# A convolution and two matrix products with an exponential between: convolutions moved, output rounds redistributed over the product steps

## Chip, cores and metric

One core of a Trainium2 chip. The time is the device time of one execution in microseconds (us); lower is better. Profiled spans are some 2 us shorter than the timed runs.

## The reference

```python
# 1. causal convolution of 7 taps, one softmaxed filter for each of 8 heads of 24 columns
#    x: (8, 4096, 192), weight: (8, 7)  ->  a: (32768, 192)
# 2. h = a @ w_in                       # (32768, 192) @ (192, 2048)
# 3. g = where(h > 0, h, exp(min(h, 0)) - 1)
# 4. out = g @ w_out                    # (32768, 2048) @ (2048, 192), float32
```

## The kernel before

It works through 32 **supersteps** of 1024 rows. A superstep has 16 **product steps**: TensorE multiplies 128 columns of w_in into one of three places in PSUM (H), ScalarE takes the exponential from there, POOL clamps it, VectorE reads the clamp and H and writes g. TensorE may write a place of H again only when VectorE has read it. Between the products TensorE does **output rounds** (two matmuls on g and w_out, side by side, from the two halves of its rows) and the **convolutions** (two for a superstep, each in two halves; each takes a place of H in turn as a product does). Outputs of half a superstep, 64 rounds, gather in one pair of banks, `ops`, which ScalarE evicts. A run of rounds has one of two sides (`turned`): which half of TensorE's rows writes which of the two banks. Before a change of side the rounds wait for the run before. In the cut below, `LAG` says at which step the rounds of a half begin, counted from the end of its superstep (-3: step 13, and step 5 of the next superstep for the other half), and each bracket of `GAPS` holds the rounds after one product.

```python
LAG = -3
GAPS = ((10,), (10,), (6,), (6,), (10,), (5, 6), (11,))   # rounds after the products of a half
CONV_AT = ((2, 1, 1), (10, 2, 0))                        # step, supersteps ahead, which convolution
EARLY_CONV = {3: (1, 0), 6: (1, 1), 9: (2, 0)}           # the first ones, by product
X_AT = ((3, 2, 1), (8, 2, 0), (11, 3, 2))                # row loads for the convolutions

    def take_slot(what):                 # the three places of H, in turn
        k = len(prior)
        prior.append(occupant[k % 3])
        occupant[k % 3] = what
        return k
# ... TensorE:
            def wait_slot(k):
                was = prior[k]
                if was is None:
                    return
                if was[0] == "h":
                    W(s_tt, 2 * was[1] + 2)        # VectorE has read that product
                else:
                    conv_read(W, was[1])
# ... TensorE, output rounds:
                                if runs[prev][0][1] != turned:
                                    W(s_swap, 2 * (prev + 1))
# ... POOL:
                for u in range(2):
                    W(s_exp, 2 * n + u + 1)
                    g.tensor_scalar(
                        out=E[:, n % NE, u, :], in0=E[:, n % NE, u, :],
                        scalar1=1.0, scalar2=0.0, op0=ALU.min, op1=ALU.max,
                    ).then_inc(s_clp)
```

Of the kernel before, what the change touches and what calls it, by code (L numbers as in the profile page):

```python
# [21 lines left out]
WPG = 5  # L22
HB = 2
BN = HB * CPH * 2 * WPG
GAP_SPLIT = 4
TAP = 6
GS = 512
SUP = 2 * GS
# [1 line left out]
NXB = 2  # L30
NE = 4
NG3 = 2
LAG = -3
GAPS = ((10,), (10,), (6,), (6,), (10,), (5, 6), (11,))
WCOLS = ((0, 256), (256, 640), (640, 1280), (1280, 2048))
Q_PART = (0,) * 2 + (1,) * 3 + (2,) * 5 + (3,) * 6
WARM = (9, 1)

CONV_AT = ((2, 1, 1), (10, 2, 0))
EARLY_CONV = {3: (1, 0), 6: (1, 1), 9: (2, 0)}  # L40
FREE_CONV = 3
QUAD = 4
XTW = 136
HALO = 2
X_AT = ((3, 2, 1), (8, 2, 0), (11, 3, 2))
X_LATE = (17, 3, 2)


def bass_lightweight_conv__then__act_elu_kernel(
# [17 lines left out]
    NS = NT // SUP  # L67
# [10 lines left out]
    def take_slot(what):  # L78
# [4 lines that stand above are left out]

    order = []

    def conv_at(s, g, gap=None):
        m = 2 * s + g - 2
        if m >= FREE_CONV:
            slot_of_conv[m] = take_slot(("c", m))
        order.append(("c", m, 0))  # L90
        between = []
        if gap:
            between, gap[:] = gap[:GAP_SPLIT], gap[GAP_SPLIT:]
        if between:
            order.append(("o", between))
        order.append(("c", m, 1))
# [4 lines left out]
    for t in range(NS):  # L101
        for half in range(2):
            at, turned = [0, 0], 0
            for i, sizes in enumerate(GAPS):
                n = NQ * (t + 1) + LAG + 8 * half + i
                gaps = []
# [28 lines left out]
    for n in range(NP):  # L135
        s, i = divmod(n, NQ)
        slot_of_pair[n] = take_slot(("h", n))
        order.append(("h", n))
        gaps = list(rounds_at.get(n, ()))
        if len(gaps) == 2:  # L140
            order.append(("o", gaps.pop(0)))
        if n in EARLY_CONV:
            conv_at(*EARLY_CONV[n])
        if s:
            for at, ahead, g in CONV_AT:
                if at == i and s + ahead < NS:
                    conv_at(s + ahead, g, gaps[0] if gaps else None)
        if gaps and gaps[0]:
            order.append(("o", gaps[0]))
    last_slot = [take_slot(None) for _ in range(2)]  # L150
    order.append(("o", tail))

# [35 lines left out]
    with ExitStack() as stack:  # L188
# [108 lines left out]
        def conv_bank(m):  # L297
            return ops if m < FREE_CONV else H[:, slot_of_conv[m] % 3, :].rearrange(
                "p (b t) -> p b t", b=2
            )  # L300
# [7 lines left out]
        def conv_read(W, m):  # L308
            W(s_ce, m + 1)
# [24 lines left out]
        @block.gpsimd  # L334
        def _gpsimd(g: bass.BassGpSimd):
            W = Waits(g)

            def load_x(s, part):
                b, t0 = s % NXB, s * SUP
                first = s % SPB == 0  # L340
                if part == 0 and not first:
                    return
                if part == 0:
                    W(s_x[b][0], x_need[s, 0])
                    g.memset(xg[0:PAD, b, 0, :], 0.0).then_inc(s_z)
                    return
                if s > NXB:
                    W(s_cv, 2 * (s - NXB))
                row = t0 + GS * (part - 1) - PAD
                v0 = WPG * (part - 1)  # L350
                whole = WPG
                if row + TOK * (WPG - 1) + P > NT:
                    whole = WPG - 1
                    rest = NT - row - TOK * whole
                    g.dma_start(
                        xg[0:rest, b, v0 + whole, :],
                        x_flat[NT - rest : NT, :],
                    ).then_inc(s_xr, 16)
                src = bass.AP(
                    tensor=x_flat.tensor,  # L360
                    offset=row * D,
                    ap=[[D, P], [TOK * D, whole], [1, D]],
                )
                g.dma_start(xg[:, b, v0 : v0 + whole, :], src).then_inc(s_x[b][part - 1], 16)  # L364

            def load_w_in(k, halves):
                c0, c1 = WCOLS[k]
                for r in halves:
                    g.dma_start(  # L369
                        w_in[HP * r : HP * (r + 1), :, c0:c1],  # L370
                        moe_w_in.rearrange("(p j) f -> p j f", j=3)[:, :, c0:c1],
                    ).then_inc(s_w[k], 16)

            W(s_one, 1)
            g.affine_select(
                out=ident[:],
                in_=ident[:],
                pattern=[[-1, P]],
                compare_op=ALU.is_equal,
                fill=0.0,  # L380
                base=0,
                channel_multiplier=1,
            ).then_inc(s_id)
            g.affine_select(  # L384
                out=sel[:].rearrange("p (r h c) -> p r h c", r=2, h=HEADS),
                in_=sel[:].rearrange("p (r h c) -> p r h c", r=2, h=HEADS),
                pattern=[[0, 2], [-1, HEADS], [0, 8]],
                compare_op=ALU.is_equal,
                fill=0.0,
                base=0,  # L390
                channel_multiplier=1,
            ).then_inc(s_id)
            W(s_wd, 16)
            load_w_in(0, (0, 1))
            load_w_in(1, (0, 1))
            load_x(1, 1)
            load_w_in(2, (0, 1))
            load_x(1, 2)
            load_w_in(3, (0,))
            load_x(2, 1)  # L400
            g.dma_start(
                w_out[:, :, :], moe_w_out.rearrange("(q p) d -> p q d", p=FC)
            ).then_inc(s_w[4], 16)
            load_x(2, 2)
            for n in range(NP):
                s, i = divmod(n, NQ)
                for at, ahead, part in X_AT:
                    if at == i and s and s + ahead < NS:
                        load_x(s + ahead, part)
                if n == X_LATE[0]:  # L410
                    load_x(*X_LATE[1:])
                for u in range(2):
                    W(s_exp, 2 * n + u + 1)
                    g.tensor_scalar(  # L414
                        out=E[:, n % NE, u, :],
                        in0=E[:, n % NE, u, :],
                        scalar1=1.0,
                        scalar2=0.0,
                        op0=ALU.min,
                        op1=ALU.max,  # L420
                    ).then_inc(s_clp)

        @block.scalar
        def _scalar(a):
# [57 lines left out]
            def conv_evac(m, b):  # L482
                s, u = m // 2 + 1, m % 2
                h0 = 4 * u + HB * b
                return a.activation(  # L485
                    csb[:, s % 2, :].rearrange(
                        "p (j v h i) -> p h j v i", j=3, v=2 * WPG, h=HEADS
                    )[:, h0 : h0 + HB],
                    conv_bank(m)[:, b, 0:BN].rearrange(
                        "p (h v i j) -> p h j v i", h=HB, v=2 * WPG, j=3  # L490
                    ),
                    ACT.Copy,
                )

            for item in order:
                if item[0] == "c":
# [7 lines left out]
                    conv_evac(m, 0)  # L504
                    if m < FREE_CONV:
                        late.append(m)
# [88 lines left out]
        def _tensor(pe):  # L595
# [16 lines left out]
            def warm_pair(count):  # L612
                for _ in range(count):
                    for r in range(2):
                        pe.matmul(  # L615
                            ops[:, r, :],
                            zw[HP * r : HP * (r + 1), 0:P],
                            zw[HP * r : HP * (r + 1), :],
                            start=True,
                            stop=True,  # L620
                            tile_position=(HP * r, 0),
                        )
# [56 lines left out]
            for x_, item in enumerate(order):  # L679
                if item[0] == "c":  # L680
# [4 lines left out]
                    else:  # L685
# [6 lines left out]
                        W(s_z, z_need[s])  # L692
                        if m < FREE_CONV:
                            conv_read(W, m - 1)
# [22 lines left out]
                elif item[0] == "h":  # L717
                    n = item[1]
                    s, q = divmod(n, NQ)
                    if n == 0:  # L720
                        W(s_ha, 2)
                        W(s_hd, 2)
                    elif n < NQ + LAG and not any(n - 2 <= e < n for e in EARLY_CONV):
                        conv_read(W, sum(e < n for e in EARLY_CONV) - 1)
                        warm_pair(WARM[1])
# [18 lines left out]
                else:  # L744
                    W(s_w[4], 16)
                    for y, (t, half, q, kb, turned) in enumerate(item[1]):
# [3 lines left out]
                        if (x_, y) in run_from:  # L750
# [7 lines left out]
                            else:  # L758
                                conv_read(W, FREE_CONV - 1)
                                W(s_oev, place[key])  # L760
# [93 lines left out]
```

## Time and profile before

Median of the four runs beside the change: 748.59 us (747.39 to 749.51).

| engine | busy, us | share of 746.5 us |
|---|---|---|
| TensorE matmuls | 731.6 | 98% |
| POOL | 664.5 | 89% |
| ScalarE | 646.8 | 87% |
| VectorE | 638.0 | 85% |

With one engine at 98% such a table cannot tell whether its work or its small waits set the time. What can is the distance from one matmul's start to the next, compared with that distance where nothing waits. The prediction shows the lines for it.

### The profile page before, as it was taken

What the parts mean: (1) busy time and instruction counts of PE and PEld (TensorE: products, weight loads), DVE (VectorE), ACT (ScalarE), POOL (GpSimd) and SP (SyncE); (2) the same over time, 40 slices, a digit from 0 to 9 for tenths busy, and PEclk for the clock granted to TensorE, in tenths of its full rate; (3) what the DMA queues carried; (4) which work ended last, traced back from release to release, by engine and by line L of the source; (5) the groups of instructions that cost most, each with busy time, mean ns of one, the idle gap of its engine ahead of it and who ended that gap; (6) DMA issues with size and microseconds to landing.
All of it is one profiled execution on the core that took longest, in us unless ns stands there. A gap on an engine that the chain in (4) does not pass through costs nothing.

```text
span 746.5 us, 28038 instructions
## 1 busy us (share of the span) xinstructions
PE 731.6 (98%) x11866; PEld 505.4 (68%) x11866; DVE 638.0 (85%) x1042; ACT 646.8 (87%) x1224; POOL 664.5 (89%) x1108
## 2 busy tenths in 40 slices
PE   6899999999999999999999999999999999999997
PEld 3466667666766676666766766766766766766666
DVE  5789889889889888898898898898898898888894
ACT  4888988988988988888989989989989989889883
POOL 8799999999899999899999899999999899898893
PEclk9999999999999999999999999999999999999999
DMA  9544435535435535345535345635345444244212
GB/s 168 93 76 91 62 70 93 94 61 92 63 68 94 93 60 95 57 74 95 82 71 94 46 84 94 77 77 70 64 91 94 67 87 81 53 89 81 46 44 66
DMA packets 132881, 58.93 MB, mean 79 GB/s; under 512 B 98068, under 2 KB 132372, under 8 KB 132756
## 3 DMA queue, kind: packets, MB, share of 16 engines
q0 software_dynamic: 44160, 17.28, 22.9%
q1 hardware_dynamic: 88308, 39.37, 21.9%
q8 instruction: 93, 1.52, 0.9%
q10 hardware_dynamic: 288, 0.49, 0.2%
q14 instruction: 32, 0.26, 0.1%
HBM read 35.61 MB, written 25.17 MB: 81 GB/s over the span
## 4 chain that ended last, share of the span: by engine, by line
PE 93%; DVE 2%; POOL 2%; DMA 1%; ACT 1%; issue 0%
PE H L735 45%; PE ops L770 44%; PE H L703 3%; DVE gT L579 2%; DMA xg<-in_x_dram 1%; ACT E L515 1%; POOL E L414 1%; PE H L770 1%; POOL w_in L369 1%; ACT csb L485 0%; POOL xg L364 0%; PE ops L703 0%; ACT osb L474 0%; PE ops L615 0%; POOL sel L384 0%
## 5 line engine op out<-in xcount | busy, mean ns | idle before, releaser
L579 DVE SCALAR_TENSOR_TENSOR gT<-E,H 128x512 f16<-128x512 f32 x1024 | 632.5, 681 | 90.9 <-POOL E L414 84.4
L414 POOL TENSOR_SCALAR E<-E 128x512 f32<-128x512 f32 x1024 | 603.9, 615 | 69.5 <-ACT E L515 62.1
L515 ACT ACTIVATE E<-H 128x512 f32<-128x512 f32 x1024 | 546.2, 608 | 73.5 <-PE H L735 64.8
L770 PE MATMUL ops<-w_out,gT 64*128 64x192 f16 x8064 | 426.4, 243 | 0.3
L770 PEld LDWEIGHTS ops<-w_out,gT 64*128 64x128 f16 x8064 | 346.9, 94 | 110.5 <-ACT osb L474 11.4
L735 PE MATMUL H<-att,w_in 64*128 64x512 bf16 x3072 | 409.2, 378 | 2.9 <-DVE gT L579 1.7
L735 PEld LDWEIGHTS H<-att,w_in 64*128 64x128 bf16 x3072 | 130.9, 94 | 111.7 <-DVE gT L579 12.8
L485 ACT ACTIVATE csb<-H 128x480 bf16<-128x480 f32 x118 | 60.9, 568 | 7.4 <-PE H L703 0.4
L474 ACT ACTIVATE osb<-ops 128x768 f32<-128x768 f32 x63 | 52.0, 826 | 6.2 <-PE ops L770 6.2
L364 POOL DMA_DIRECT2D xg<-in_x_dram x62 | 55.7, 899 | 0.1
L703 PE MATMUL H<-xg,Tm 64*128 64x240 bf16 x472 | 44.0, 263 | 0.1
L703 PEld LDWEIGHTS H<-xg,Tm 64*128 64x128 bf16 x472 | 21.2, 94 | 0.8 <-DVE gT L579 0.3
L485 ACT ACTIVATE csb<-ops 128x480 bf16<-128x480 f32 x6 | 3.5, 588 | 3.2 <-PE ops L703 3.2
L770 PE MATMUL H<-w_out,gT 64*128 64x192 f16 x128 | 5.9, 243 | 0.0
L703 PE MATMUL ops<-xg,Tm 64*128 64x240 bf16 x24 | 2.7, 306 | 3.3 <-DMA xg<-in_x_dram 3.1
L590 DVE COPY osb<-H 128x192 f32<-128x192 f32 x1 | 0.4, 358 | 6.3 <-PE H L770 6.3
L770 PEld LDWEIGHTS H<-w_out,gT 64*128 64x128 f16 x128 | 5.3, 94 | 0.0
L369 POOL DMA_DIRECT2D w_in<-in_moe_w_in_dram x7 | 4.6, 663 | 0.3 <-DMA wh<-in_weight_dram 0.3
L610 PE MATMUL ops<-zw 128*128 128x512 bf16 x9 | 3.6, 577 | 1.2 <-DVE zw L527 1.2
L615 PE MATMUL ops<-zw 64*128 64x512 bf16 x12 | 2.4, 381 | 2.3 <-ACT csb L485 2.3
L703 PEld LDWEIGHTS ops<-xg,Tm 64*128 64x128 bf16 x24 | 0.9, 97 | 5.2 <-issue 3.5
L615 PEld LDWEIGHTS ops<-zw 64*128 64x128 bf16 x12 | 0.6, 93 | 4.2 <-ACT csb L485 3.9
(49 smaller groups left out, 26.3 us busy)
## 6 DMA issues: line engine op xcount, KB each, us to landing
out_dram<-osb SPq DMA_DIRECT2D x126, 192.0 KB, 4.1
xg<-in_x_dram POOLq DMA_DIRECT2D x61, 240.0 KB, 5.6
w_out<-in_moe_w_out_dram POOLq DMA_DIRECT2D x1, 768.0 KB, 16.1
att<-csb SPq DMA_TRANSPOSE x31, 6.4
w_in<-in_moe_w_in_dram POOLq DMA_DIRECT2D x2, 240.0 KB, 9.0
xf<-in_x_dram ACTq DMA_DIRECT2D x1, 384.0 KB, 3.2
xf<-in_x_dram SPq DMA_DIRECT2D x1, 384.0 KB, 3.6
w_in<-in_moe_w_in_dram POOLq DMA_DIRECT2D x2, 144.0 KB, 4.2
```

Source lines behind the costliest of these rows:

```text
L364: g.dma_start(xg[:, b, v0 : v0 + whole, :], src).then_inc(s_x[b][part - 1], 16)
L369: g.dma_start(w_in[HP * r : HP * (r + 1), :, c0:c1], moe_w_in.rearrange("(p j) f -> p j f", j=3)[:, :, c0:c1],).then_inc(s_w[k], 16)
L414: g.tensor_scalar(out=E[:, n % NE, u, :], in0=E[:, n % NE, u, :], scalar1=1.0, scalar2=0.0, op0=ALU.min, op1=ALU.max,).then_inc(s_clp)
L474: a.activation(osb[:, b, :, :, :].rearrange("p g k d -> p g (k d)"), ops[:, :, 0 : 2 * D], ACT.Copy,).then_inc(s_oev)
L485: return a.activation(csb[:, s % 2, :].rearrange("p (j v h i) -> p h j v i", j=3, v=2 * WPG, h=HEADS)[:, h0 : h0 + HB], conv_bank(m)[:, b, ...
L515: a.activation(E[:, n % NE, u, :], H[:, k, GS * u : GS * (u + 1)], ACT.Exp).then_inc(s_exp)
L579: v.scalar_tensor_tensor(out=gT[:, s % NG3, q, u, :], in0=E[:, n % NE, u, :], scalar=1.0, in1=H[:, slot_of_pair[n] % 3, GS * u : GS * (u + ...
L610: pe.matmul(ops[:, 0, :], zw[:, 0:P], zw[:], start=True, stop=True)
L615: pe.matmul(ops[:, r, :], zw[HP * r : HP * (r + 1), 0:P], zw[HP * r : HP * (r + 1), :], start=True, stop=True, tile_position=(HP * r, 0),)
L703: ins = pe.matmul(to[:, b, n1 * hh : n1 * (hh + 1)], Tm[HP * rt : HP * (rt + 1), h, :], xg[HP * rt : HP * (rt + 1), s % NXB, :, :].rearran ...
L735: ins = pe.matmul(H[:, k % 3, GS * r : GS * (r + 1)], w_in[HP * r : HP * (r + 1), j, FC * q : FC * (q + 1)], att[HP * r : HP * (r + 1), s ...
L770: ins = pe.matmul(acc[:, g, d0 : d0 + D], gT[HP * rt : HP * (rt + 1), t % NG3, q, g, t0 : t0 + P], w_out[HP * rt : HP * (rt + 1), q, :], s ...
```

## The change

It is meant to keep apart the two extra jobs of ScalarE, the convolution's eviction and the output's: the convolutions go half way between the output evictions, and the rounds are dealt anew over the steps. (`FREE_CONV` counts the first convolutions, which write `ops` and take no place of H.)

```diff
-LAG = -3
-GAPS = ((10,), (10,), (6,), (6,), (10,), (5, 6), (11,))
+LAG = -4
+GAPS = ((), (8,), (11,), (6, 5, 4), (7,), (1,), (9,), (13,))
-CONV_AT = ((2, 1, 1), (10, 2, 0))
-EARLY_CONV = {3: (1, 0), 6: (1, 1), 9: (2, 0)}
-FREE_CONV = 3
+CONV_AT = ((7, 1, 1), (15, 2, 0))
+EARLY_CONV = {6: (1, 0), 8: (1, 1)}
+FREE_CONV = 2
-X_AT = ((3, 2, 1), (8, 2, 0), (11, 3, 2))
-X_LATE = (17, 3, 2)
+X_AT = ((0, 2, 1), (6, 2, 0), (8, 2, 2))
 ... (in the order of a step)
+        if convs and len(gaps) == 3:
+            order.append(("o", gaps[0]))
+            conv_at(*convs[0], gaps[1])
+            order.append(("o", gaps[2]))
+            continue
```

## The prediction

> **What bounds the kernel now.** I read the page first, then the timeline of one steady half, then the waits, then the start.
>
> ```profile
> span 746.5 us, 28038 instructions
> PE 731.6 (98%) x11866; PEld 505.4 (68%) x11866; DVE 638.0 (85%) x1042; ACT 646.8 (87%) x1224; POOL 664.5 (89%) x1108
> ...
> PE H L735 45%; PE ops L770 44%; PE H L703 3%; DVE gT L579 2%; DMA xg<-in_x_dram 1%; ACT E L515 1%; POOL E L414 1%; PE H L770 1%; POOL w_in L369 1%; ACT csb L485 0%; POOL xg L364 0%; PE ops L703 0%; ACT osb L474 0%; PE ops L615 0%; POOL sel L384 0%
> ```
>
> TensorE is busy 98% and is 93% of the chain, but three engines stand behind it at 85 to 89%. So the question is what TensorE loses inside its own row. The timeline of TensorE shows that (start, length, line, count):
>
> ```profile
> 223.27 1.46 PE L735 MATMUL H<-att,w_in 64*128 64x512 bf16 x12
> 224.56 0.99 PE L770 MATMUL ops<-w_out,gT 64*128 64x192 f16 x20
> 225.39 0.81 PE L735 MATMUL H<-att,w_in 64*128 64x512 bf16 x6
> ...
> 231.44 0.57 PE L770 MATMUL ops<-w_out,gT 64*128 64x192 f16 x10
> 231.85 0.37 PE L703 MATMUL H<-xg,Tm 64*128 64x240 bf16 x4
> 232.10 0.50 PE L770 MATMUL ops<-w_out,gT 64*128 64x192 f16 x8
> 232.44 0.37 PE L703 MATMUL H<-xg,Tm 64*128 64x240 bf16 x4
> ...
> 234.46 1.46 PE L735 MATMUL H<-att,w_in 64*128 64x512 bf16 x12
> ```
>
> Lengths overlap, so I take starts from starts. A product step costs (224.56 - 223.27)/2 = 0.648 us; an output round, two matmuls side by side, (225.39 - 224.56)/10 = 0.0825 us; a half convolution of 4 matmuls 0.205 us, and 0.25 us if the output rounds after it have changed sides (231.85 to 232.10). A half (8 steps, 64 rounds, one convolution) has 8 x 0.648 + 64 x 0.0825 + 0.41 = 10.87 us of work. The two halves from this point take 11.19 (234.46 - 223.27) and 11.31 us, mean 11.25. Loss: 0.38 us a half, over 64 halves 24 us of 749, which is all that a reordering in steady state can win. Who takes it, in the waits of the stretch from 84.4 to 732 us:
>
> ```profile
> PEld ops L770 <- ACT osb L474: 10.7, 58, 0.2
> PEld H L735 <- DVE gT L579: 8.0, 35, 0.4
> ...
> PEld ops L770 <- PE ops L770: 4.3, 25, 0.3
> ```
>
> The first costs nothing: it is a weight load that waits beside the two products of the empty step (after the x12 line the rounds begin 1.29 us later, exactly two products). The second is the real one: a product may start only when VectorE has read what lay in its one of three H places. The third is the change of sides.
>
> The length of that ring decides. Here is one product with every engine behind it free:
>
> ```profile
> 252.95 3.81 DVE L579 SCALAR_TENSOR_TENSOR gT<-E,H 128x512 f16<-128x512 f32 x6
> ...
> 253.29 0.81 PE L735 MATMUL H<-att,w_in 64*128 64x512 bf16 x6
> ...
> 254.15 1.09 ACT L515 ACTIVATE E<-H 128x512 f32<-128x512 f32 x2 [0.39 <-PE H L735]
> ...
> 254.82 1.19 POOL L414 TENSOR_SCALAR E<-E 128x512 f32<-128x512 f32 x2 [0.18 <-ACT E L515]
> ```
>
> Product at 253.29, VectorE done at 252.95 + 3.81 = 256.76: **3.47 us**, and some 0.06 until TensorE restarts, so 3.53. Any stretch of TensorE's order between a product and the one three H places later must last 3.53 us, or TensorE stands. The convolution takes an H place too, which shortens the stretch around it.
>
> **What the Trainium skill says.** "TensorE: Matmul & The Clock Gate", Back-to-back issue gap, gives columns/2.4 + 2.5 ns: 216 ns for 512 and 82.5 for 192. The trace agrees: 1.29/6 = 0.215 and 0.0825 us. So the row is at its rate wherever nothing waits. "PSUM — Partial Sum Buffer", PSUM bank collisions, says that different row tiles may not use one bank at once; that is why rounds that swap sides wait for the run before, and the trace shows that as the 0.25 against 0.205. "Perfetto Trace Analysis", Identifying the Most-Contended Engine, calls matmul busy time a bad metric and prefers the weight loads' share; 68% here, yet only 3.4% of the row can be won, so neither number alone decides and I go by starts. The clock gate section of the first page says that an idle window of about 3.4 us halves the clock; here the table by stretches has the clock at 1.00 from 38.5 us to 732, and 0.94 between 10.8 and 38.5, so it matters at the start alone.
>
> **The change, part by part.** Removed and added work: none in matmuls, evictions or bytes. Every half still has 64 rounds, one convolution, 8 products, 9 runs of rounds. What moves: rounds per step from 10,10,6,6,10,5+4+2,11,0 (steps 13, 14, 15, 0, 1, 2, 3, 4, and again 5 to 12) to 0,8,11,6+5+4,7,1,9,13 (steps 12 to 3, and 4 to 11); the convolution from step 2 to step 15 (10 to 7); the row loads from steps 3 and 11 to 0 and 8.
>
> (1) Convolution. Before, one of its two borders had rounds that change sides; now 6, 5, 4 alternate, so both do: 0.05 + 0.01 us more a half, on the path.
>
> (2) Ring. TensorE's time by step afterwards: step 12: 0.65; 13: 0.648 + 8 x 0.0825 = 1.31; 14: 1.56; 15: 0.648 + 15 x 0.0825 + 0.51 = 2.40; 0: 1.23; 1: 0.73; 2: 1.39; 3: 1.72. Stretches between users of one H place:
> - 0 to 3: 1.23 + 0.73 + 1.39 = 3.35 against 3.53, so 0.17 us is lost whatever the other engines do. Step 1 with its single round is the cause.
> - 12 to 15: 0.65 + 1.31 + 1.56 = 3.52. ScalarE takes product 12 late because it evicts the output just before (the same delay is in the trace: product at 245.77, VectorE done at 249.36, ring 3.59), so 3.65 is needed: short by 0.13.
> - 2 to 5 (the next half's second step, as 13): 1.39 + 1.72 + 0.65 = 3.76; but product 2 follows 1 after only 0.73 us while ScalarE needs 0.97 for one (3.10/3 in the trace) and POOL 1.15, so its ring is 3.93: short by about 0.2, less what earlier standing gives back.
> - 13 to the convolution: 4.01, against 4.08 + 0.06 for the second of two products back to back. 14 to 0, 15 to 1, 1 to 4 and 3 to 6 fit (3.95, 3.62, 3.84, 3.68).
> Carrying each engine's free time from step to step by hand (0.97, 1.15 and 1.20 us a product for ScalarE, POOL and VectorE; 1.02 more where POOL starts a row load; 0.92 and 0.69 on ScalarE for convolution and output) the standing settles at 0.17 + 0.06 + 0.06 + 0.05 = 0.34 us a half. With two changes of sides 0.12, and 0.035 for weight loads that come late, 0.50 against 0.38 before. The same walk on the order of before gives 11.20 for the half measured as 11.19.
>
> So steady state becomes slower: 0.12 x 2 = 0.23 us a superstep, over about 29.5 of them +6.8 us. The memset before each new batch now falls on step 6, where POOL is already late: an estimated 7 x 0.15 = +1. At the end the 6, 5, 4 stand without a convolution between: +0.3.
>
> (3) Start. Here the change gives something back:
>
> ```profile
> 18.33 1.23 PE L703 MATMUL ops<-xg,Tm 64*128 64x240 bf16 x8 [3.05 <-DMA xg<-in_x_dram]
> ...
> 20.10 0.72 SPq L802 DMA_DIRECT2D w_in<-w_in  x1
> ```
>
> Before, the first convolution is at step 3 and TensorE stands 3.05 us for its rows. Now it is at step 6, which VectorE's pace (1.2 us a product after the fourth at 14.45) puts at 18.05, and the rows have landed. But step 10 needs the last columns of w_in, whose copy starts at 20.10 and lands after 6.3 us (table of DMA issues), 26.4. So step 10 starts near 26.4 instead of 28.16; carried on, superstep 1 begins near 35.2 instead of 38.5, with 8 rounds more done (0.66). The wait of 0.82 us in step 19 (two row loads close together) should go too. Together -4.8 us.
>
> Sum: 749.2 + 6.8 + 1 + 0.3 - 4.8 = **752.5 us**.
>
> **The rivals.** (A) The intent works: ScalarE's two extra jobs, now half a half apart, no longer pile up and the ring never closes. For it: ScalarE, POOL and VectorE all lag exactly where both fall together now. Then the loss falls to the changes of sides, 0.12, saving 0.26 x 64 = 17, and with the start it would be about 728 us. Against it: the 3.35 us between 0 and 3 is below the ring with all engines free, so it cannot vanish. (B) A late transfer: the transposition now follows a convolution in step 7 instead of 2. From there to the next superstep there are about 13.8 us; convolution, eviction and the slowest landing (8.3 us) need 11.5. Were it to miss by 1 us, 30 supersteps would make 780. Rows asked for in step 8 have seven steps, as now; they land in 5.5. I hold this unlikely. (C) Only the start counts and the ring is as before: 744.
>
> **Range and chances.** The steady term is uncertain by about 5 us (0.08 us a half, as the halves of before differ by 0.1), the start by 2. So 746 to 758. Faster by 2% means 734, which needs A in full; slower by 2% means 764, which needs B or twice my ring loss.
>
> **What would show it.** In the profile after: halves of 11.3 to 11.4 us where 11.25 was; TensorE's rounds of step 2 followed by a product that waits some 0.17 us for VectorE, in nearly every half; both convolution borders at 0.25; superstep 1 beginning at 35 +- 2 us and no 3 us wait for rows. Wrong if the half is under 11.2, if a wait for the transposition or rows shows in each superstep, or if rounds wait for ScalarE after the empty step.

## The result

754.33 us median (752.03 to 754.69, 4 runs) against 748.59. Ratio 1.0071, interval 1.0045 to 1.0097: 0.7% slower, inside 2%. (A ratio is the mean of one kernel's runs over the mean of the other's of the same rounds, so not quite the ratio of the medians.)

Taking the starts of products from both traces says where the 5.6 us between the profiled spans (746.5 and 752.1) lie:

| stretch | before, us | after, us | difference |
|---|---|---|---|
| start of product 0 to product 32 | 48.47 | 47.62 | -0.85 |
| product 32 to product 496 (29 supersteps) | 653.27 | 659.54 | +6.27 |
| product 496 to the end | 34.02 | 34.24 | +0.22 |

The loss is spread evenly over the steady state: 22.71 us a superstep in the median, in place of 22.51. The timeline of TensorE after the change, one steady half (start, length, line, count):

```profile
222.81 1.48 PE L733 MATMUL H<-att,w_in 64*128 64x512 bf16 x12
...
228.83 0.81 PE L733 MATMUL H<-att,w_in 64*128 64x512 bf16 x6
229.48 0.74 PE L768 MATMUL ops<-w_out,gT 64*128 64x192 f16 x14
230.06 0.81 PE L733 MATMUL H<-att,w_in 64*128 64x512 bf16 x6
230.71 0.25 PE L768 MATMUL ops<-w_out,gT 64*128 64x192 f16 x2
230.79 0.81 PE L733 MATMUL H<-att,w_in 64*128 64x512 bf16 x6
231.44 0.91 PE L768 MATMUL ops<-w_out,gT 64*128 64x192 f16 x18
232.36 0.82 PE L733 MATMUL H<-att,w_in 64*128 64x512 bf16 x6
...
234.09 1.50 PE L733 MATMUL H<-att,w_in 64*128 64x512 bf16 x12
```

The product at 228.83 is that of step 8, which corresponds to step 0 of the other half; 230.06, 230.79 and 232.36 are steps 9, 10 and 11. Nine rounds from 231.44 are through after 9 x 0.0825 = 0.74 us, at 232.18; the next product starts at 232.36. From the product at 228.83 to that one, three places on in the ring, are 3.53 us, the length of the ring to the hundredth. In the half beside it (steps 0 to 7) the same stretch lasts 3.60 in the median, because VectorE there finishes product 0 in 3.54 in place of 3.47 us.

The waits of the stretch from 84.4 to 732 us, after:

```profile
PEld H L733 <- DVE gT L577: 36.5, 114, 0.7
...
PEld ops L768 <- PE ops L768: 5.5, 32, 0.3
```

The product's wait for VectorE rose from 8.0 us in 35 groups to 36.5 in 114. (The weight load waits partly beside a matmul that still runs, so these are not all lost; the starts give the loss.) No group of this stretch waits for a transfer, and the wait for ScalarE's output eviction of before is gone.

The start (TensorE's timeline, after):

```profile
18.70 0.84 PE L701 MATMUL ops<-xg,Tm 64*128 64x240 bf16 x8
...
25.86 1.46 PE L733 MATMUL H<-att,w_in 64*128 64x512 bf16 x6 [2.30 <-DMA w_in<-w_in]
```

The first convolution no longer waits for its rows; product 10 instead stands 2.30 us for the copied columns of w_in.

### The profile page after: what moved, and what is told of

Same layout as the page of the kernel before. It is cut to its first block, busy times and chain, and to the rows that moved or that the text cites. A ratio compares the mean times of both kernels' runs of the same rounds, so it can differ in the third digit from the quotient of the medians.

```text
span 752.1 us, 28042 instructions
## 1 busy us (share of the span) xinstructions
PE 736.1 (98%) x11868; PEld 494.5 (66%) x11868; DVE 630.7 (84%) x1042; ACT 649.1 (86%) x1224; POOL 661.4 (88%) x1108
## 4 chain that ended last, share of the span: by engine, by line
PE 79%; DVE 6%; ACT 5%; POOL 4%; issue 3%; DMA 2%; DVEq 0%; ACTq 0%
PE H L733 37%; PE ops L768 37%; DVE gT L577 6%; PE H L701 4%; POOL E L412 3%; ACT E L513 3%; ACT csb L483 2%; DMA w_in<-in_moe_w_in_dram 2%; DMA w_in<-w_in 1%; PE H L768 1%; POOL w_in L369 1%; POOL xg L364 0%; DVEq L277 0%; POOL xg L355 0%; PE ops L613 0%
## 5 line engine op out<-in xcount | busy, mean ns | idle before, releaser
L577 DVE SCALAR_TENSOR_TENSOR gT<-E,H 128x512 f16<-128x512 f32 x1024 | 625.2, 682 | 103.8 <-POOL E L412 66.9
L513 ACT ACTIVATE E<-H 128x512 f32<-128x512 f32 x1024 | 535.5, 607 | 66.2 <-PE H L733 56.6
L768 PEld LDWEIGHTS ops<-w_out,gT 64*128 64x128 f16 x8064 | 340.8, 94 | 109.8 <-PE ops L768 6.8
L733 PEld LDWEIGHTS H<-att,w_in 64*128 64x128 bf16 x3072 | 126.8, 94 | 128.2 <-DVE gT L577 44.2
L701 PEld LDWEIGHTS H<-xg,Tm 64*128 64x128 bf16 x480 | 19.0, 94 | 8.0 <-issue 4.8
```

Source lines behind the costliest of these rows:

```text
L513: a.activation(E[:, n % NE, u, :], H[:, k, GS * u : GS * (u + 1)], ACT.Exp).then_inc(s_exp)
L577: v.scalar_tensor_tensor(out=gT[:, s % NG3, q, u, :], in0=E[:, n % NE, u, :], scalar=1.0, in1=H[:, slot_of_pair[n] % 3, GS * u : GS * (u + ...
L701: ins = pe.matmul(to[:, b, n1 * hh : n1 * (hh + 1)], Tm[HP * rt : HP * (rt + 1), h, :], xg[HP * rt : HP * (rt + 1), s % NXB, :, :].rearran ...
L733: ins = pe.matmul(H[:, k % 3, GS * r : GS * (r + 1)], w_in[HP * r : HP * (r + 1), j, FC * q : FC * (q + 1)], att[HP * r : HP * (r + 1), s ...
L768: ins = pe.matmul(acc[:, g, d0 : d0 + D], gT[HP * rt : HP * (rt + 1), t % NG3, q, g, t0 : t0 + P], w_out[HP * rt : HP * (rt + 1), q, :], s ...
```

## The experiments

Two theories stood after the result. **The ring**: a product can start only when the one three places earlier has gone through ScalarE, POOL and VectorE, 3.53 us, and the new deal makes stretches of TensorE's order shorter than that. **Placement and side changes**: what matters is where the convolutions stand beside ScalarE's evictions, and how often rounds change sides. For the start and end the question was how much they give or take.

### Two more rounds in the thin step

```diff
-GAPS = ((), (8,), (11,), (6, 5, 4), (7,), (1,), (9,), (13,))
+GAPS = ((), (8,), (11,), (6, 5, 4), (6,), (3,), (10,), (11,))
```

> The changed kernel with the rounds of steps 0, 1, 2, 3 set to 6, 3, 10, 11 in place of 7, 1, 9, 13; convolutions, loads and all else as in the change. Theory (the ring of three H places closes because step 1 holds one round): the stretch from product 0 to product 3 grows from 3.35 to 3.51 us (0.648 x 3 + 19 x 0.0825), so the stand there shrinks from 0.23 to some 0.05 us and the half from 11.355 to about 11.20; over 61 halves -9.5 us, 745 (743 to 747). Rival (the place of the convolutions, or the side changes around them, carry the loss): both are untouched, so 754. Rival (start and end carry it): 754.

747.55 us (before 748.19 in the same rounds; ratio 0.9995, 0.998 to 1.0011). The half is 11.24 and 11.28 us by turns, in place of 11.355. Equal times do not mean equal stretches: this run's trace has product 32 at 57.43 us, against 59.23 before, so a part of the time came from the start. From product 32 to 496 it takes 653.84 us, so 0.57 us of the 6.27 are left. The steady loss thus nearly vanishes without a convolution, a load or a side change being moved. The expectation of 745 was missed, because a part of the gain turned up elsewhere, in the two products of the empty step (its timeline):

```profile
252.56 0.81 PE L733 MATMUL H<-att,w_in 64*128 64x512 bf16 x6
253.20 1.07 PE L768 MATMUL ops<-w_out,gT 64*128 64x192 f16 x22
254.11 1.62 PE L733 MATMUL H<-att,w_in 64*128 64x512 bf16 x12
255.57 0.82 PE L768 MATMUL ops<-w_out,gT 64*128 64x192 f16 x16
```

From 254.11 to 255.57 are 1.46 us, where two products need 1.295: the second waits 0.165. Its place was that of product 2. The stretch from there holds one round less than in the change (10 + 11 in place of 9 + 13), and the stand before product 3, which lies in it, is shorter by 0.165.

### One more round in the thin step

```diff
-GAPS = ((), (8,), (11,), (6, 5, 4), (7,), (1,), (9,), (13,))
+GAPS = ((), (8,), (11,), (6, 5, 4), (7,), (2,), (9,), (12,))
```

> The changed kernel with 7, 2, 9, 12 in place of 7, 1, 9, 13: one round moved from step 3 to step 1, half the dose of the other. Theory of the ring: the stretch from product 0 to 3 grows by one round, 0.0825 us, so the stand there shrinks by that and the half becomes about 11.27; over 61 halves -5 us, 749.3 (748 to 751). The rivals say 754.

748.12 us (ratio to before 0.9999), the half 11.28 us. With the other two runs this is a series. Mean time that TensorE stands, from the starts, steps 0 to 7:

| rounds in step 1 | before product 3 | before product 5 | half, us |
|---|---|---|---|
| 1 (the change) | 0.263 | 0.014 | 11.355 |
| 2 | 0.182 | 0.096 | 11.277 |
| 3 | 0.099 | 0.179 | 11.26 (mean of its two halves) |

Each round moved takes 0.08 us from the first stand, one round's length, and gives 0.08 to the second. The half still gains from the first move, because a wait of 0.065 us further on (before product 7) goes with it. That is how a ring behaves, and the rivals have nothing that would.

### The convolutions alone, half way

```diff
-GAPS = ((10,), (10,), (6,), (6,), (10,), (5, 6), (11,))
-CONV_AT = ((2, 1, 1), (10, 2, 0))
+GAPS = ((10,), (10,), (6, 5), (6,), (6,), (10,), (11,))
+CONV_AT = ((7, 1, 1), (15, 2, 0))
```

(The kernel before, with the row loads of the change.)

> The kernel before with its convolutions alone put half way between the output evictions (steps 15 and 7, row loads at 0, 6 and 8 as in the change), its rounds 10,10,6+5,6,6,10,11,0 so that the step with the convolution keeps 11 rounds. If putting the convolutions half way helps ScalarE, as the change intends, this is faster than before: 745 or less. Theory of the ring: the stretch from product 15 to product 1, with the convolution in it, is 0.648 x 2 + 17 x 0.0825 + 0.46 = 3.16 us against 3.53 needed, so it stands some 0.3 us more there and the half takes about 11.42 in place of 11.25: +10 us, 759 (756 to 763).

757.58 us, ratio 1.013 (1.0114 to 1.0145), halves of 11.36 and 11.51 us. The place of the convolution is thus no gain by itself in this deal (the 11 rounds of its step went with it, so the deal is not quite that of before; a worth of the place in every deal is not shown either way). The stand is where the ring says, at the product behind it:

```profile
252.86 0.37 PE L700 MATMUL H<-xg,Tm 64*128 64x240 bf16 x4
253.07 0.25 PE L767 MATMUL ops<-w_out,gT 64*128 64x192 f16 x2
253.61 0.82 PE L732 MATMUL H<-att,w_in 64*128 64x512 bf16 x6 [0.29 <-DVE gT L576]
```

One round is through at 253.15; the product starts at 253.61. The steps around the convolution had been left thin. In a kernel whose convolutions move, the rounds must move with them, which is what the change did at steps 7 and 15 but undid at step 1.

### The ring made shorter

```diff
-                for u in range(2):
-                    W(s_exp, 2 * n + u + 1)
-                    g.tensor_scalar(out=E..., in0=E..., ..., op0=ALU.min, op1=ALU.max).then_inc(s_clp)
+                W(s_exp, 2 * n + 2)
 ... VectorE:
-                    W(s_clp, 2 * n + u + 1)
+                    W(s_exp, 2 * n + u + 1)
```

(The changed kernel; the result is wrong where h is positive, relative error 0.026.)

> The changed kernel with POOL's clamp taken out: VectorE takes the exponentials straight from ScalarE, so the result is wrong on purpose where h is positive. Nothing on TensorE, no eviction and no transfer changes; only the ring gets shorter, by POOL's 0.65 us (3.53 to 2.88). Theory of the ring: every stretch of the order (the shortest is 3.35) is then long enough, the stands for VectorE vanish in steady state, and the half falls from 11.355 to about 11.0 (work 10.87 and 0.1 for side changes and double waits): -0.35 x 61 = -21 us, 733 (729 to 738). If ScalarE's pile of work or TensorE's own row is what holds it, little changes: 750 or more.

731.29 us, ratio to before 0.9773 (0.9756 to 0.979). All halves are 10.99 us: 10.87 of work and 0.12 around the convolution. TensorE's timeline at the same place as above:

```profile
254.44 0.81 PE L724 MATMUL H<-att,w_in 64*128 64x512 bf16 x6
255.08 0.74 PE L759 MATMUL ops<-w_out,gT 64*128 64x192 f16 x14
255.66 0.81 PE L724 MATMUL H<-att,w_in 64*128 64x512 bf16 x6
256.31 0.25 PE L759 MATMUL ops<-w_out,gT 64*128 64x192 f16 x2
256.39 0.81 PE L724 MATMUL H<-att,w_in 64*128 64x512 bf16 x6
257.04 0.91 PE L759 MATMUL ops<-w_out,gT 64*128 64x192 f16 x18
257.78 0.81 PE L724 MATMUL H<-att,w_in 64*128 64x512 bf16 x6
```

257.78 - 254.44 = 3.34 us, the bare work that the prediction gave this stretch. With POOL's step out of the ring every stand is gone, though ScalarE is now busy 89% of the span. So ScalarE with all its evictions is not what bounds the row here. The edit takes away POOL's work (88% busy) along with its share of the trip, and cannot tell the two apart; the two runs before it, in which POOL's work is unchanged, show that the deal of rounds counts. What a perfect deal could win at most is shown as well: the same order with no stand is 23 us below the change (754.33 to 731.29, not of the same rounds).

### The first convolutions alone

```diff
-EARLY_CONV = {3: (1, 0), 6: (1, 1), 9: (2, 0)}
+EARLY_CONV = {6: (1, 0), 8: (1, 1), 11: (2, 0)}
```

(The kernel before, else unchanged.)

> The kernel before with only its first three convolutions moved: after products 6, 8 and 11 in place of 3, 6 and 9, steady state untouched. The prediction gave the start 4.8 us; the trace of the changed kernel shows only 0.87 us gained by product 32, and that the prediction took product 18 of before (38.5 us) for product 16 (35.9). If that misreading is the whole error, the three microseconds of waiting for rows at product 3 go here too, but are mostly taken back at product 10, which waits for the last columns of w_in until about 25.9: product 16 at 35.0 to 36.0, total 747 to 748.5, within 1 us of before. If the early convolutions had the large gain that was forecast, product 16 would come near 31 to 32 and the time near 744.

746.88 us against 748.42, ratio 0.9978 (0.9966 to 0.9991): a real but small gain, of some 1.5 us, just under the 747 to 748.5 expected, with product 16 at 35.04 in place of 35.90 in its trace. The forecast of 4.8 us for the start cannot be had by this. One trace is a weak witness here. Six profiled kernels with the late first convolutions and the copied columns of w_in (the change, its repetition, the first two experiments, this one and the next) had product 16 at 34.98 to 37.41 us. In each of the six, product 10 starts 0.04 to 0.05 us after the copy lands, at 25.25 to 27.51 us. The latest was the repetition. It and the change take the same 9.86 us from product 10 to 16, so the 1.69 us between them lay in the landing (27.51 and 25.81), and not in the clock between 26 and 40 us, which was 0.77 and 0.89.

### The end

```diff
+    for n in (NP - 17, NP - 9, NP - 1):
+        first, turned_part, rest = rounds_at[n]
+        rounds_at[n] = [first + rest]
+        rounds_at[n + 1] = [turned_part + rounds_at[n + 1][0]]
```

(The changed kernel. These three halves have no convolution any more between 6, 5 and 4 rounds.)

> The changed kernel with the three last convolution-less halves (steps 495, 503, 511) given 10 rounds of one side in place of 6, 5, 4; the 5 of the other side join the next step's rounds. In the changed trace the 6, 5, 4 without a convolution between them stood 0.53 us in each of these three steps, two side changes of 0.26 us, where before had one in each of two halves. If that is a cost of neighbouring side changes alone, 3 x 0.53 = 1.6 us go: 0.2% below the changed kernel of the same rounds, about 752.5. If it is merely a wait that some other one replaces, nothing changes. Steady state stays at 11.37 us a half.

> The changed kernel itself, unchanged, as the comparison for e6_tail on the same chip and in the same rounds: 754 (752 to 755).

751.75 us, and the changed kernel again 753.38 in the same rounds (ratios to before 1.0046 and 1.0070). By these ratios they differ by 0.24%, as expected, but the two ranges overlap (751.38 to 753.17 and 752.68 to 755.79), so the traces are the better witness: product 480 to the end takes 56.87 us in the repetition, 56.86 in the change and 55.10 in this one, 1.77 us less. TensorE's timeline at the step in question in the change, and then that step and the next in this experiment:

```profile
727.47 1.93 PE L768 MATMUL ops<-w_out,gT 64*128 64x192 f16 x30
729.24 0.81 PE L733 MATMUL H<-att,w_in 64*128 64x512 bf16 x6
```

```profile
726.12 0.99 PE L773 MATMUL ops<-w_out,gT 64*128 64x192 f16 x20
726.95 0.81 PE L738 MATMUL H<-att,w_in 64*128 64x512 bf16 x6
727.60 1.15 PE L773 MATMUL ops<-w_out,gT 64*128 64x192 f16 x24
728.59 0.81 PE L738 MATMUL H<-att,w_in 64*128 64x512 bf16 x6
```

15 rounds need 1.24 us and took 1.77: two changes of side with nothing between them cost 0.53 us, 0.26 each. The experiment's 10 rounds of one side took 0.83 = 10 x 0.0825, and the 12 of the next step, five of them moved there, 0.99 = 12 x 0.0825. The move also changed the ring: the stands before products 499 and 507 (0.25 and 0.17) went, and waits of 0.23 came in the empty steps 500 and 508, where at most 0.05 had been; these nearly cancel. A half convolution between leaves 0.05 of such a change, a whole product nothing.

### All together

The rounds 6, 3, 10, 11, the end as just shown, and w_in loaded whole from memory:

```diff
-            load_w_in(3, (0,))
+            load_w_in(3, (0, 1))
-            sy.dma_start(w_in[HP:P, :, c0:c1], w_in[0:HP, :, c0:c1]).then_inc(s_wc, 16)
```

> Rounds 6, 3, 10, 11 as in the first experiment (747.5), the end as in e6_tail, and the last columns of w_in loaded whole from memory in place of half of them copied within the core, so that product 10 waits less. Start: the copy began at 20.1 and landed near 25.9; a second load should land near 22 to 23, so product 10 comes at some 23.5 and product 16 1 to 2 us earlier than 35.0. End: 1.6 us. Sum -2.6 to -3.6 on the first experiment: 744.4 (743 to 746), 0.5% below before. If the loads of the start merely delay each other, 746.

744.58 us against 748.42, ratio 0.9939 (0.9925 to 0.9953): the fastest correct kernel, by 0.6% over before. Its start is the uncertain part. Product 10 no longer waits for a transfer, but the profiled run was with 747.45 the slowest of its seven, and had product 16 only at 36.97. Its trace shows a delay well before product 10 (VectorE's copy of the taps for the convolution, then TensorE; after them VectorE in the changed kernel):

```profile
12.54 3.73 DVE L574 COPY Tm<-Tr 128x1024 bf16<-128x1024 bf16 x1 [1.79 <-DMA Tr<-conv_taps]
17.52 0.82 PE L734 MATMUL H<-att,w_in 64*128 64x512 bf16 x6 [3.91 <-DVE gT L581]
...
12.15 0.43 DVE L570 COPY Tm<-Tr 128x1024 bf16<-128x1024 bf16 x1 [1.51 <-DMA Tr<-conv_taps]
```

That copy took 3.73 us, against 0.42 to 0.73 in the other nine traces, and held product 3 until 17.52, where the change has it at 14.43. POOL's clamps ran beside it from 12.47 to 15.98 us; that they held it was not tested. So this trace says little on the load of w_in. The clock of 0.79 from 18 to 26 us is no mark of it: before had the same there. How much of the gain is the load of w_in was not tested by itself.

## Why the prediction was right, and where not

- **The ring.** Right, and shown from both sides: longer stretches take the stand away round by round, a shorter ring takes away all of it. For the stretch 0 to 3 the prediction had 0.17 us; measured were 0.19 and 0.26 in the two halves, and at least 0.17 in each of the 58 halves of the steady stretch. Of the other short stretches, which it settled at 0.06 (2 to 5), 0.06 (12 to 15) and 0.05 (13 to the convolution), 2 to 5 stood only 0.01 and 0.03 in the two halves, 12 to 15 and 4 to 7 stood 0.05 and 0.06, and the convolutions 0.13 and 0.04. The half was 11.355 in the median, 11.37 in the mean, just what 0.50 of loss on 10.87 of work make. That the sum fits better than its terms is partly luck: the stretch 0 to 3 and the convolution of step 15 stood longer than forecast, 2 to 5 and the side changes less. (Its 0.97 us for ScalarE is written as 3.10/3, which is 1.03; from start to start the trace has 0.48 to 0.50 us an activation, two to a product, so 0.97 stands.)
- **Side changes.** The step "both borders at 0.25" failed in its first part: only the second border shows 0.05. Before the first, the convolution itself waits for its place, and the change of side is over by then; in the run with the shorter ring, where it does not wait, both borders show 0.05. With the 0.01 of other side changes the term is 0.06 in step 15 and 0.08 in step 7, instead of 0.12.
- **Steady sum.** +6.8 and +1 for the memset were foreseen, +6.27 measured over 29 supersteps. The memset costs nothing new: 0.08 us a batch after, 0.07 before.
- **The end.** +0.3 came out near, but not by its own reason. The three unseparated steps stand 0.53 us each, 1.6 in sum. They come out at +0.22 after product 496 since one of them lies ahead of it, before had two single side changes of 0.26 there, and eight rounds (0.66 us) are done earlier, while the ring's stands there add some 0.37.
- **The start.** This step failed: "superstep 1 begins near 35.2 instead of 38.5". The 38.5 us of before belong to product 18; product 16 began at 35.90. The forecast for after was good (35.72), the wait for the w_in copy came as told (26.4 foreseen, 25.86 measured), and the wait of step 19 went (superstep 1: 23.33 to 22.64). But the gain to product 16 was 0.7 by the prediction's own numbers, not 3.3. With that, its start would have been -2.2 and its sum 755.1, against 754.33 measured. The range held since the error was smaller than it, and the total came near partly by luck: start and end together were forecast 3.9 us too good (-4.5 against -0.63), steady state with the memset 1.5 us too bad (+7.8 against +6.27). The change forecast was +3.3 (from 749.2, which is 0.6 above the median of before); measured are +5.7.
- **The rivals.** (A), that the intent works and the ring never closes, is refuted: the stand before product 3 or 11 appears in every half of the steady stretch, and the convolutions alone cost 1.3%. (B), a late transfer, does not occur: no wait for rows or for the transposition in steady state. (C), only the start counts, is refuted by the +6.27.

The trace shows where VectorE loses 0.07 us at product 0: it starts 0.105 us after POOL's clamp there and 0.035 at product 8, in the median. Product 0 is the one product of a superstep before which its code waits for a second semaphore (for the output rounds of the superstep two before, done five steps earlier). That this wait is the cause was not tested. Open are also why the copy of w_in lands up to 2.3 us apart in the profiled runs, and why the copy of the taps once took 3.73 us.

## What to carry to other kernels

Where several engines hand a product round through a few buffers, write down the time of one round trip with every engine free, then add up the bound engine's work between each user of a buffer and the next user of that buffer: every sum must exceed the trip. The trip is longer for a product close behind another, which finds the engines busy: 3.98 us to the end of VectorE's work for product 2 of the change, 0.73 us behind product 1, where product 8 takes 3.47. Work that fills such stretches is best dealt evenly; a round taken from one stretch lengthens another, so a local gain can turn up as a new wait one step on. And count products in the trace before comparing two of them: an index off by two made the largest error of this prediction, 2.6 us.

## What the Trainium skill lacked or had wrong

- "TensorE: Matmul & The Clock Gate", Back-to-back issue gap, gives about 131 ns as the spacing of 512-column matmuls in a stream with weight loads and calls the formula's 216 ns too high there. Here each of two row tiles that work side by side had a weight load and a 512-column matmul every 215.8 ns. So the formula held for each tile, and 131 was not seen. (But for nine at the start, no matmuls on the whole array run here to set against it.)
- "PSUM — Partial Sum Buffer", PSUM bank collisions, names the rule for row tiles but no page gives the price of keeping it by semaphore: 0.26 us for neighbouring changes of side, 0.05 with a half convolution between, none with a product between.
- "Perfetto Trace Analysis", Identifying Dependency Chains, says that an instruction that waits on several engines may get additional wait instructions, and gives no cost. In the change the convolution of step 15, which waits for three semaphores, started 0.146 us after VectorE had freed its place, that of step 7 with one 0.057; VectorE's 0.105 and 0.035 above are a second such pair. That the waits are the cause was not tested.
- No page found says how far one transfer's landing differs between executions: the copy of w_in's last columns (288 KB) landed 5.96 us after its issue in one profiled run of the change and 6.80 in the other, and had been issued 0.86 later; product 16 came 1.69 us later.
